# One more seven-product group in the first layer of the third half batch, with a newly written issue order

## The chip, the cores and the metric

One core of one Trainium2 chip. The metric is the time of one execution on the device in microseconds (us); lower is better. Work runs on TensorE (PE in the profile; PEld is its weight load), VectorE (DVE), ScalarE (ACT) and GpSimd (POOL); SyncE (SP) only issues transfers here.

## The reference

Attention over q, k, v of 4 x 8 x 768 x 64 (batch, heads, tokens, head size), in which a token sees the 8 first tokens (global) and itself with the 95 before it (local); then a feed-forward block with a squared ReLU on the 3072 tokens, with w_in 512 x 2048 and w_out 2048 x 512:

```python
scores = scale * np.matmul(q, k.transpose(0, 1, 3, 2))
bias = -slopes[:, None, None] * dist[None, :, :]
scores = np.where(keep, scores + bias[None], -1000000000.0)
a = softmax(scores)
x = np.matmul(a, v)          # then 3072 tokens x 512
h = np.maximum(x @ w_in, 0.0)
out = h * h @ w_out          # 3072 x 512, float32
```

## The kernel before

**Half batches.** The tokens are worked in eight half batches of 384 (H0 to H7). Each goes through the same stages: its q, k and v are loaded in tiles of 128 tokens; q and k are transposed so that the head size lies on the partitions; scores are made on TensorE (`score_unit`, L715, 64 rows of the array at a time), turned into exponentials on ScalarE (L728, ex) and masked on VectorE (phat); `attend` (L776) multiplies them with v and divides; the result tm is transposed by a transfer into xt (L801). Then the first layer (hps) and the second layer (yps, L1145 and L1059), whose sums y are stored. The stages of neighbouring half batches interleave: while H2 runs through its first layer, H3 makes scores and H4 is being loaded.

**First layer, two ways.** The 16 hidden blocks of 128 are made either plainly or in groups. A plain job (`layer1`, L822) makes one block: four matmuls over 384 columns (tokens), a relu out of the bank (L847 on ScalarE or L849 on VectorE), and a square for two blocks. A group (`layer1_group`, from L911) makes four blocks, two "near" and two "far", by seven block products in place of eight, after Strassen and Winograd: the columns are cut in halves of 192, the input channels in halves, and products p1 to p7 run on sums of weights (in_mix) and of tokens (x_mix) that are made ahead, once for all groups. A product is four matmuls over 192 columns (L925). Sums that several outputs share are held: `keep` copies a bank into a tile kept (L353 on ScalarE, L355 on VectorE). `give` makes hr from a bank: with a relu alone (L989 or L991), or adding a held sum first (add_relu, a custom instruction of VectorE, L983). In H2 groups are "seeded" (SEEDS): p1, p5, p6, p3, p7, p2, p4 in this order, with keep1 after p1, keep5 after p5, keep2 after p6, add_relu after p3 and p7, plain relus after p2 and p4, and a copy that writes keep1 back into p3's bank (seed) before p2 adds to it. So a seeded group has eight evacuations out of or into banks.

**Which jobs are in groups** is a string for each half batch, LAYER1 (L46). A letter of "abcdefg" is a product of group 3, of "ABCDEFG" of group 2, a digit of group 1; "s" is a plain job. Group 0's blocks are always plain.

**What sets the order.** One list of all engines' work, ORDER (L54 to L119), is read by `by_table` (L256): each word is an engine's letter and a number (p: the next TensorE job of that number, l: a load, others: any other operation), after a dot the banks, and after an @ the operation that a load must wait for. Every engine takes its work strictly in this order. So a wait holds up everything behind it on the same engine.

**Loads and transposes of q and k.** The transposes k<-sk and q<-sq are transfers that SyncE issues (`turn_by_dma`, L666 to L697, issue L670). Their sources sk and sq have one buffer each, so the loads of the next half batch (GpSimd's queue, `list_loads`, L491) wait for the transposes of the half batch before. The transpose that is issued first also waits for the last load of sq (x.last_load). The transpose of H4, for instance, must land before H4's first score. The values of a half batch also need a version vb in which the global tokens stand (`fix_v` L596, `fix_globals` L618); some of it is copied by transfers from SyncE, `vb<-v` (L625; L608 and L609 in `values_by_dma`).

```python
if not x.turns:
    behind(turn, x.last_load)            # turn_by_dma
for turn in halves[x.hb - 1].turns + (prev.xturns if AFTER[x.hb] else []):
    behind(dma, turn)                    # list_loads, tile 0 of sk
```

Of the kernel before, what the change touches and what calls it, by code (L numbers as in the profile page):

```python
# [45 lines left out]
LAYER1 = {2: "sasbcsdABCsesDEsFGfsgs", 3: "as123456b7cdsAeBCfgDsEFsG",  # L46
# [7 lines left out]
ORDER = """d1 s8 g2 a4 p0.0 a6 s10 d12 a0 d13 l1 d3 l4 l2 l3 d146 a26 d15 d20 a22 l0 a30 d9 d21 a18 d5 a17  # L54
a16 d14 a19 p1.12 a27 p5.34 a28 d11 l5 a29 p10.56 l9 d7 a23 l7 p3 l8 p4.7 l6 d32 a31 a24 d37 p6
d33 a34 p2.07 a39 d35 d36 p7 a40 p11 l10 a25 a41 p8.2 d43 p9.1 p13.34 a46 p12.20 d44 p17 l11 a42
d45 p14.1 d59 a47 l12 p15 d48 a52 p16.5 p24.7 p19.6 d51 p20.3 a49 l13 d55 a53 p18.1 p21.2 d64 l14
a50 p28.5 p23.64 d56 d38 a69 p27.7 d54 l16 p31.0 a57 p26.5 p34.32 a60 d72 l17 p29.6 d68 a61 p35.1
d70 p22.0 d58 l15 l18 a81 p25.4 p30.3 a85 p36.7 d65 a82 p39.16 a86 d71 a66 p32.02 a92 p33.47 d67
d63 p40.35 a77 d84 d91 p38.1 a78 d83 d62 d80 p37.4 l19 a73 d79 a74 p44.7 l22 p41.0 a93 d107 d87  # L60
d76 p47.2 a97 p52.6 p45.7 a89 l21 l23 d111 l20 l27 d96 a119 p48.3 a98 d75 l28 a101 p46.4 l29 p43.1
d110 p53.6 p42.2 d105 l30 d95 p50.5 p55.0 a103 l25 p49.4 d116 d94 a120 a112 p59.1 l24 a102 d88
d106 a90 p51.5 a108 d189 p60.2 a114 d100 a104 d99 p56.6 a113 d191 a122 p57.3 p65.7 d125 p54.4 d138
a117 p63.0 p62.5 a128 d121 a109 p58.1 d139 d129 d130 p61.3 a118 p67.7 d115 a132 d133 d272 a131
p70.4 a135 p71.2 a126 a142 p72.3 p69.0 d162 d127 p82.5 d190 a156 d192 a165 p66.1 a159 l31 a157
a160 p64.7 d205 d158 l26 d163 a123 d161 p84.0 d134 a140 d206 l36 d143 a166 p83.4 d207 a136 l35
d164 p81.6 a167 d187 a141 p85 l33 d124 a137 d186 p79.21 l34 l32 a184 d147 p88.37 p80.45 a178 p77.6
a195 p74.2 a181 d201 d202 a196 d204 p68.3 d203 a179 d151 a182 p73.4 d208 d180 a144 p90.7 l39 d183
a145 p86 a174 a168 d152 a169 p75.1 d154 p78.53 d153 p89.64 p87 a175 d148 a198 p100.2 a176 d155
a193 d150 p98.5 l38 p91.6 a185 d197 a199 d228 p76.3 a209 d177 a210 l37 p96.0 s229 a171 d200 p92  # L70
d172 d225 a173 s194 p93.5 s216 p94 d170 a188 d149 a211 p95.4 d236 s217 p105.1 d219 p97 d214 d237
d212 s220 p102.3 a240 p104 a245 p103.0 s226 d213 d238 a244 d227 d223 d221 p101 d218 p106 l45 a222
p99 l41@226 d246 a241 s215 d243 p109.54 p110.70 s224 l44 a234 p108.36 a251 d239 p111 d258 p118.5
a252 a248 a249 d250 p107 d273 p116.43 p113 a255 l42 p112 a268 l43@217 a256 d253 d230 d254 p119.6
l40 d257 d231 a269 p114.74 l47 p115.03 p124 a261 d274 l46 s235 p120 a283 d259 a264 d270 s275
p122.6 a262 p129.7 d280 p121.2 s242 s325 a265 d232 p127.0 d267 p126 d276 a287 p133.4 d285 d295
a286 d263 s324 p117.3 a290 d233 p130 p123.1 a278 p140 d266 a271 p132 d281 a307 p135 a291 p134.4
p128.2 d298 p136 d294 a279 p131.3 d300 s282 a299 s247 p137.6 a308 l48@324 a297 p138 a303 d323 d301
p139 p125.1 a302 p142 d288 d304 a292 p143.4 d305 a310 d311 p141.6 d326 l49 s296 a284 a312 p144.7
a309 d293 s289 l52 a306 p145.23 d313 p146.05 p147.14 l50 a327 d318 p148.6 a333 d433 d319 a322 l54  # L80
p149.2 a330 d336 a328 d314 l53 p151.16 d320 a331 p150.03 p152 a337 d329 l51 a338 d332 p157.5 a339
p153 d321 a341 d316 a344 a350 a334 p172.0 l65 d315 a342 d345 p159.3 d340 p158.1 p161 d335 a355
p164.2 a352 p155.4 d370 p154.6 p163 a347 d351 s371 p168.0 d395 p162 p169.1 d317 d358 a364 p156
a348 s398 p174.0 d356 a366 d343 a365 p171.4 d359 s399 l56 p177 p160.3 s277 d369 a378 p165 l55 a360
p167 d357 s346 d353 a363 p173.2 p166.4 a372 p178.5 a362 s260 d373 p175 d349 a361 p180 d375 p182.3
s374 p179 d382 a379 p176 p170 d380 p183 d385 p181.0 a381 s354 p184 a376 a383 s386 p185.5 d367 d400
a387 p186.23 d384 a389 p188.46 d388 l60@371 p187.01 a368 d377 a413 l59@354 p189.7 a406 d401 d405
l57 a414 d402 p190.4 a409 d404 l62 d403 a407 p191 a410 l63 p193.26 a417 d416 a418 p194.03 d415
p192.17 l61@386 p195 d476 d411 a419 s390 d391 a426 d408 l58 p196 p206.1 d393 a422 p198.0 d397 a420
p197.2 a434 d396 l74 a423 p219.7 d392 a432 d412 a427 d394 p210 d480 d429 p218.6 a445 d477 a462  # L90
d424 p208 a461 p204.4 d431 a448 p205.3 d421 p215.1 a444 p203.7 d443 p214 d442 a458 s491 l66 p199.6
p217.4 d457 p209 a451 p220 d435 a463 p202.7 d449 s492 d428 a441 p212.6 p224 a446 d454 p201 p207.3
a460 d481 d425 s436 a439 p200.7 d482 a471 p221 a447 p213 p216.6 d437 p222.5 d456 s438 d459 d478
# [1592 lines left out]
```

## Time and profile before

| | us |
|---|---|
| median of 3 runs | 201.74 (201.61 to 205.66) |
| the profiled execution | 201.98 |
| its span | 200.2 |
| PE / PEld busy | 191.8 / 160.8 |
| DVE / ACT / POOL busy | 177.7 / 146.3 / 66.6 |

The span is the time between the first and the last event in the profile; the execution has some microseconds around it. Busy time is summed per engine; PEld overlaps PE. The chain names the work that ended last, step by step back from the end. A window is a stretch of the span with the busy time of each engine in it. A row of a timeline gives start, duration, engine, line, operation, output<-input and, in brackets, the idle time of that engine before it and what ended it. SPq and POOLq are the queues in which SyncE and GpSimd issue transfers.

### The profile page before, as it was taken

Reading aid. Unit: us, or ns where it says so; the run is one execution under the profiler, and the core shown is the slowest. Engines: PE = TensorE matmul, PEld = TensorE weight load, DVE = VectorE, ACT = ScalarE, POOL = GpSimd, SP = SyncE. Lnnn points to the kernel's source line nnn. Section 1 sums busy time; section 2 is a strip of 40 time slices with the busy share of each in tenths; the row PEclk is TensorE's granted clock in tenths of the full one; section 3 lists DMA queues with packets and bytes.
Section 4 is the critical chain, followed back from the end, with each engine's and each line's share of the span. In section 5 each row is a group of like instructions: output and inputs, shape, how many; then the busy total and the mean of one; then the engine's idle time right before and its main releaser. Section 6 shows DMA issues by size and latency. Waiting matters only on the chain.

```text
span 200.2 us, 5881 instructions
## 1 busy us (share of the span) xinstructions
PE 191.8 (96%) x2349; PEld 160.8 (80%) x2349; DVE 177.7 (89%) x448; ACT 146.3 (73%) x310; POOL 66.6 (33%) x82
## 2 busy tenths in 40 slices
PE   7797999999999999999999998999999999999993
PEld 3575899856888687789877897889879899889992
DVE  6889778999995989999999997999999899899780
ACT  6899857998836679988888758987986866365311
POOL 5998537537102910970108700670000000000000
PEclk9999999999999999999999999999999999999999
DMA  5999999999998999999999995699734420020214
GB/s 161 177 149 181 198 181 171 207 194 155 149 224 89 143 123 243 134 149 105 272 119 93 152 140 114 146 150 155 199 75 142 105 75 2 0 108 0 108 52 157
DMA packets 106987, 27.52 MB, mean 137 GB/s; under 512 B 97104, under 2 KB 104016, under 8 KB 106960
## 3 DMA queue, kind: packets, MB, share of 16 engines
q0 software_dynamic: 74944, 13.11, 87.4%
q1 hardware_dynamic: 30816, 13.45, 32.1%
q10 hardware_dynamic: 1200, 0.59, 1.1%
q8 instruction: 18, 0.29, 0.7%
q14 instruction: 9, 0.07, 0.2%
HBM read 27.26 MB, written 6.29 MB: 168 GB/s over the span
## 4 chain that ended last, share of the span: by engine, by line
PE 76%; DMA 13%; POOL 6%; DVE 3%; issue 1%; SPq 0%; ACT 0%; POOLq 0%; DVEq 0%
PE yps L1145 29%; PE hps L822 17%; PE hps L925 17%; DMA w_in_sb<-in_moe_w_in_dram 5%; PE sp L715 4%; PE av L776 4%; PE yps L1059 4%; DMA q<-sq 3%; DMA xt<-tm 3%; DMA v<-in_v_dram 3%; POOL w_mix L491 2%; POOL v L491 2%; DVE hr L983 1%; PE trp L650 1%; POOL sk L491 1%
## 5 line engine op out<-in xcount | busy, mean ns | idle before, releaser
L822 PE MATMUL hps<-xt,w_in_sb 128*128 128x384 f16 (+2 forms) x336 | 45.3, 281 | 0.8 <-DMA w_in_sb<-in_moe_w_in_dram 0.8
L728 ACT ACTIVATE ex<-sp 128x512 f16<-128x512 f32 x66 | 35.3, 619 | 4.4 <-PE sp L715 3.6
L1145 PEld LDWEIGHTS <-h 128*128 128x128 f16 x376 | 34.1, 98 | 4.7
L822 PEld LDWEIGHTS <-w_in_sb 128*128 128x128 f16 x336 | 28.0, 98 | 8.7 <-DMA w_in_sb<-in_moe_w_in_dram 1.2
L1145 PEld LDWEIGHTS <-mixed 128*128 128x128 f16 x272 | 25.1, 98 | 3.1 <-DVE mixed L1110 0.2
L847 ACT ACTIVATE hr<-hps 128x384 f16<-128x384 f32 (+1 forms) x43 | 21.7, 548 | 7.6 <-PE hps L822 7.6
L983 DVE CUSTOM_DVE_ANT_0 hr<-hps,kept 128x384 f16<-128x384 f32 x49 | 25.8, 549 | 1.1 <-PE hps L925 0.7
L491 POOL DMA_DIRECT2D sq<-in_q_dram x19 | 17.0, 900 | 27.2 <-DMA xt<-tm 13.2
L353 ACT COPY kept<-hps 128x384 f32<-128x384 f32 x43 | 20.3, 491 | 7.9 <-PE hps L925 5.8
L353 ACT COPY y<-yps 128x256 f32<-128x256 f32 (+2 forms) x36 | 12.7, 381 | 18.0 <-PE yps L1145 16.5
L491 POOL DMA_DIRECT2D v<-in_v_dram x24 | 21.6, 918 | 12.1 <-DMA k<-sk 9.6
L491 POOL DMA_DIRECT2D sk<-in_k_dram x19 | 17.1, 902 | 25.2 <-DMA xt<-tm 9.4
L925 PEld LDWEIGHTS <-in_mix 128*128 128x128 f16 x272 | 23.0, 98 | 2.4 <-DVE x_mix L903 0.5
L925 PE MATMUL hps<-x_mix,in_mix 128*128 128x192 f16 x204 | 23.7, 247 | 0.2 <-DVE x_mix L903 0.2
L1145 PE MATMUL yps<-w_mix,h 128*128 128x256 f16 (+1 forms) x192 | 22.7, 264 | 0.0
L1145 PE MATMUL yps<-w_out_sb,h 128*128 128x256 f16 (+1 forms) x184 | 22.5, 268 | 0.0
L1145 PE MATMUL yps<-w_mix,mixed 128*128 128x256 f16 (+1 forms) x184 | 22.3, 268 | 0.0
L752 DVE TENSOR_TENSOR phat<-ex,mask 128x1024 f16<-128x1024 f16 (+1 forms) x36 | 21.0, 594 | 0.1
L1005 ACT ACTIVATE h<-hr 128x768 f16<-128x768 f16 x22 | 18.5, 848 | 1.2 <-DVE hr L983 0.7
L925 PEld LDWEIGHTS <-w_in_sb 128*128 128x128 f16 x204 | 17.4, 98 | 1.5
L861 ACT ACTIVATE h<-hr 128x768 f16<-128x768 f16 (+1 forms) x23 | 17.0, 768 | 1.7 <-DVE hr L849 0.9
L925 PE MATMUL hps<-xt,w_in_sb 128*128 128x192 f16 x136 | 15.8, 246 | 0.0
(110 smaller groups left out, 347.9 us busy)
## 6 DMA issues: line engine op xcount, KB each, us to landing
out_dram<-y SPq DMA_DIRECT2D x23, 256.0 KB, 2.6
v<-in_v_dram POOLq DMA_DIRECT2D x24, 128.0 KB, 6.4
sk<-in_k_dram POOLq DMA_DIRECT2D x19, 128.0 KB, 6.0
sq<-in_q_dram POOLq DMA_DIRECT2D x19, 128.0 KB, 5.0
w_in_sb<-in_moe_w_in_dram POOLq DMA_DIRECT2D x4, 512.0 KB, 10.2
w_out_sb<-in_moe_w_out_dram POOLq DMA_DIRECT2D x4, 512.0 KB, 10.5
y<-in_k_dram ACTq DMA_DIRECT2D x2, 256.0 KB, 4.8
y<-in_q_dram SPq DMA_DIRECT2D x2, 256.0 KB, 4.2
```

Source lines behind the costliest of these rows:

```text
L353: nc.scalar.copy(out=out, in_=in_)
L491: dma = nc.gpsimd.dma_start(out=dst, in_=src[x.b, :, r0 + t * P:r0 + (t + 1) * P, :] .rearrange("h p d -> p h d"))
L715: nc.tensor.matmul(sp[h][:, i, :], lhsT=lhsT, rhs=x.q[rows, r % HT, a, :], start=True, stop=True)
L728: nc.scalar.activation(out=st["ex"][:, h], in_=sp[h], func=AF.Exp, scale=scale)
L752: eng(e).tensor_tensor(out=x.phat[a][:, :, t0:t0 + n], op=ALU.mult, in0=st["ex"][:, :, i0:i0 + 2 * n].rearrange("p e (t b) c -> p e t (b c ...
L822: nc.tensor.matmul(st["ps"][:, i * n:(i + 1) * n], lhsT=w_in_sb[:, kk, m * P:(m + 1) * P], rhs=x.xt[:, kk, c0:c1], start=kk == 0, stop=kk ...
L847: nc.scalar.activation(out=o, in_=i, func=AF.Relu)
L861: nc.scalar.activation(out=h2, in_=hr, func=AF.Square)
L925: nc.tensor.matmul(st[name][:, i * HC:(i + 1) * HC], lhsT=left(i, kk), rhs=right(kk), start=fresh and i == kk == 0, stop=kk == KK - 1, ski ...
L983: nc.vector._custom_dve(TENSOR_ADD_SAT, out=hidden(which)[:, :, cols], in0=sums(name), in1=st[kept], s0=LARGEST, s1=0.0)
L1005: nc.scalar.activation(out=h2, in_=hr, func=AF.Square)
L1145: nc.tensor.matmul(st[bank_name][:, 0:n], lhsT=a(m), rhs=b(m)[:, cols], start=fresh and m == 0, stop=m == HK - 1, skip_group_check=not fresh)
```

## The change

H2 gets group 1 as well, in place of four plain jobs: 18 groups in all, for 17. The word for H2 now has three groups and four plain jobs. ORDER is written anew for all engines, one line longer, so all lines behind it have a number higher by one in the changed kernel (L822 is L823, and so on). 25 loads have an @ in it, where 8 had one. The core of the diff:

```diff
-LAYER1 = {2: "sasbcsdABCsesDEsFGfsgs", 3: "as123456b7cdsAeBCfgDsEFsG",
+LAYER1 = {2: "1a2b3csd4ABC5es6DEs7FGfsg", 3: "as123456b7cdsAeBCfgDsEFsG",
...
-ORDER = """d1 s8 g2 a4 p0.0 a6 s10 d12 a0 d13 l1 d3 l4 l2 l3 d146 a26 d15 d20 a22 l0 a30 d9 d21 a18 d5 a17
```

Counted over the kernel: matmuls of hps over 192 columns 476 to 504, over 384 columns 144 to 128; copies into kept 51 to 54, seed copies 2 to 3, add_relus 49 to 51, relus over 2 x 192 19 to 21, relus over 384 36 to 32. Several other copies move between ScalarE and VectorE.

**First place: GpSimd's loads of H4.** The rows are loads in order; the brackets name the semaphores that a load waits for. DMAHW0 to DMAHW7 are those of SyncE's transfers, taken in turn; DMASW0 to 7 are GpSimd's own. Before:

```order
L491 DMA sq<-in_q_dram 128x8x64 [waits DMASW3_49,DMAHW7_49,DMASW1_49,DMASW0_49]
L491 DMA sk<-in_k_dram 128x8x64 [waits DMAHW1_49,DMAHW6_49,DMASW4_49,DMASW2_49]
L491 DMA sq<-in_q_dram 128x8x64
L491 DMA sk<-in_k_dram 128x8x64
L491 DMA sq<-in_q_dram 128x8x64
L491 DMA sk<-in_k_dram 128x8x64 [waits DMASW5_49]
```

The changed kernel:

```order
L492 DMA sk<-in_k_dram 128x8x64 [waits DMAHW4_49,DMAHW6_49,DMASW4_49,DMAHW7_49,DMASW2_49,DMASW0_49]
L492 DMA sq<-in_q_dram 128x8x64 [waits DMAHW2_49,DMASW3_49,DMASW1_49]
L492 DMA sq<-in_q_dram 128x8x64
L492 DMA sk<-in_k_dram 128x8x64 [waits DMAHW0_49]
L492 DMA sk<-in_k_dram 128x8x64
L492 DMA sq<-in_q_dram 128x8x64 [waits DMASW5_49]
```

One load goes ahead of the gate in both. The gate of the second was an xt transpose of H2 (DMAHW1), and is now the copy vb<-v of H3 (DMAHW2), which SyncE issues behind it. The last load of sq, which the first transpose of H4 waits for, was the fourth of the loads behind the first, and is now the last.

**Second place: SyncE around the transposes of H7.** Before:

```order
L670 DMA_TRANSPOSE k<-sk 128x12x128 [waits DMASW7_49,DMASW5_49,DMAHW0_49,DMASW1_49,DMASW0_49]
L670 DMA_TRANSPOSE q<-sq 128x12x128 [waits DMASW6_49,DMAHW1_49,DMASW4_49,PE_49]
L1230 DMA out_dram<-y 128x512 [waits DMAHW2_49,DVE_49]
L1230 DMA out_dram<-y 128x512 [waits DMAHW3_49,Activation_49]
L801 DMA_TRANSPOSE xt<-tm 128x3x128 [waits DMAHW4_49,DVE_49,PE_49]
```

The changed kernel:

```order
L671 DMA_TRANSPOSE k<-sk 128x12x128 [waits DMASW6_49,DMASW5_49,DMAHW0_49,DMASW1_49,DMASW0_49]
L609 DMA vb<-v 96x520 [waits DMAHW1_49,DMASW2_49]
L610 DMA vb<-v 32x520 [waits DMAHW2_49]
L671 DMA_TRANSPOSE q<-sq 128x12x128 [waits DMASW7_49,DMAHW3_49,DMASW4_49,PE_49]
L1231 DMA out_dram<-y 128x512 [waits DMAHW4_49,DVE_49]
L1231 DMA out_dram<-y 128x512 [waits DMAHW5_49]
L802 DMA_TRANSPOSE xt<-tm 128x3x128 [waits DMAHW6_49,DVE_49,PE_49]
```

The two copies vb<-v stood behind the xt transposes that follow; now they stand between k and q, and the first of them waits for a v load (DMASW2).

**Third place: ScalarE in H2's first layer.** kept<-hps holds a sum, hps<-kept is the seed copy, hr<-hps a relu and h<-hr a square. Before:

```order
L353 COPY kept<-hps 128x384
L353 COPY hps<-kept 128x384
L353 COPY kept<-hps 128x384
L847 ACTIVATE hr<-hps 128x384 x2
L989 ACTIVATE hr<-hps 128x2x192
L353 COPY kept<-hps 128x384
L861 ACTIVATE h_1436<-hr 128x768
L353 COPY hps<-kept 128x384
L1005 ACTIVATE h_1436<-hr 128x768
```

The changed kernel:

```order
L354 COPY kept<-hps 128x384
L862 ACTIVATE h_1440<-hr 128x768
L990 ACTIVATE hr<-hps 128x2x192
L354 COPY hps<-kept 128x384
L1006 ACTIVATE h_1440<-hr 128x768
L354 COPY kept<-hps 128x384 x2
L990 ACTIVATE hr<-hps 128x2x192
L354 COPY kept<-hps 128x384
L848 ACTIVATE hr<-hps 128x384
L990 ACTIVATE hr<-hps 128x2x192
L354 COPY hps<-kept 128x384
```

Two of the three seed copies stay with ScalarE, the third goes to VectorE; between them stand more copies into kept and fewer plain relus.

More of the change, by code (lines that the diff above doesn't have):

```diff
@@ L59 @@
[L59 to L82, printed above, removed]
@@ L89 @@
[L89 to L93, printed above, removed]
-p211 a464 d489 l64 p223 d467 a469 p227.2 a484 a493 p229.7 d452 p225 d465 p230 s455 l70@455 d483
@@ L122 @@
+s729 d759 p369 a758 p363 p372 p373 p371.5 a757 d747 d742 s743 d751 d762 d761 d760 p376 p375 a768
+s763 d766 a769 s767 p366 a754 p374 s755 d764 s765"""
 class Op:
```

100 lines of the change are left out of this document (65 added, 35 removed).

## The prediction

> **What bounds the kernel now.** I read the page first: its span, the busy shares, then the chain that ended last by engine and by line.
>
> ```profile
> span 200.2 us, 5881 instructions
> PE 191.8 (96%) x2349; PEld 160.8 (80%) x2349; DVE 177.7 (89%) x448; ACT 146.3 (73%) x310; POOL 66.6 (33%) x82
> PE 76%; DMA 13%; POOL 6%; DVE 3%; issue 1%; SPq 0%; ACT 0%; POOLq 0%; DVEq 0%
> ```
>
> TensorE is busy for 191.8 of 200.2 us, and 76% of the chain is its work. A change can pay in two ways only: less matmul time, or less of the 8.4 us in which TensorE idles. The windows say where that idle time is. The columns are the stretch, its length, then PE, PEld, DVE, ACT and POOL busy, the granted clock, the DMA share and GB/s.
>
> ```profile
> 60.00:70.00 10.00, 10.00 (x121) 7.33 (x120) 7.60 (x19) 6.73 (x15) 6.35 (x8) 1.00 1.20 116
> 70.00:80.00 10.00, 10.00 (x116) 8.04 (x115) 9.00 (x24) 8.56 (x19) 0.65 (x1) 1.00 1.57 181
> 100.00:110.00 10.00, 9.84 (x120) 7.68 (x115) 9.83 (x25) 8.73 (x21) 4.29 (x5) 1.00 1.13 108
> 110.00:120.00 10.00, 9.85 (x139) 9.21 (x137) 9.79 (x26) 6.56 (x15) 3.63 (x5) 1.00 1.92 146
> 120.00:130.00 10.00, 9.43 (x117) 7.84 (x115) 8.62 (x22) 8.98 (x19) 3.21 (x4) 1.00 0.69 130
> ```
>
> Of the idle time most lies in the start, where the first weights land, and in the end, behind the last matmul; the change reaches neither, but for the last evacuation. In the middle three stretches miss 0.16, 0.15 and 0.57 us. The stretch in which the third half batch (H2; they are numbered from H0) has its first layer, 60 to 80, misses nothing: what is saved there is saved only if the evacuations and the transfers keep pace. The chain names what TensorE stood for in 110 to 130: a transposed q.
>
> ```profile
> 115.92 0.81 PE hps L925 x10
> 116.73 5.47 DMA q<-sq
> 122.20 0.14 issue
> 122.34 0.62 PE sp L715 x16
> ```
>
> The score runs of H6 start at 122.34, when a transpose that was issued at 116.73 has landed. So the transfers that bring q and k are the second limit: wherever TensorE comes to a score run early, or a transpose late, a stall appears.
>
> **The matmuls.** A plain job of the first layer is four matmuls over 384 columns, a block product four over 192. Two pieces of the chain inside the stage price them.
>
> ```profile
> 74.85 0.65 PE hps L822 x4
> 75.86 0.33 PE hps L925 x4
> ```
>
> Four plain jobs go, 4 x 0.65 = 2.60; seven products come, 7 x 0.33 = 2.31. The sums of weights and of tokens that they read are made already for every half batch that has groups, so nothing else is added. **-0.29.** Both kinds run here at the pace of their columns (0.163 and 0.082 per matmul), with their weight loads beside them. The Trainium skill ("TensorE: Matmul & The Clock Gate", section "Back-to-back issue gap") speaks against that: it puts streams of weight load and matmul at about 81 ns for 128 columns and about 131 ns for 512. An estimate by it, drawn straight between those two, is 89 ns for 192 columns and 114 for 384, so 28 x 89 - 16 x 114 would make the group dearer by 0.67 us; the rows above disagree with it.
>
> **The evacuations.** Four relus of 384 columns go. The new group, of the seeded kind that H2 uses, holds three sums (a copy each), adds two held sums with a relu, writes one held sum back and takes two plain relus: 8 for 4. The squares stay two.
>
> ```profile
> L353 ACT COPY kept<-hps 128x384 f32<-128x384 f32 x43 | 20.3, 491 | 7.9 <-PE hps L925 5.8 <-DVE hr L983 1.6
> L983 DVE CUSTOM_DVE_ANT_0 hr<-hps,kept 128x384 f16<-128x384 f32 x49 | 25.8, 549 | 1.1 <-PE hps L925 0.7 <-ACT h L1005 0.2
> L353 ACT COPY hps<-kept 128x384 f32<-128x384 f32 x2 | 1.0, 482 | 0.5 <-DVE hr L983 0.5
> L847 ACT ACTIVATE hr<-hps 128x384 f16<-128x384 f32 x29 | 13.4, 508 | 5.3 <-PE hps L822 5.3
> ```
>
> That is 3 x 0.491 + 2 x 0.549 + 0.482 + 2 x 0.508 less 4 x 0.508: +2.04 us on ScalarE and VectorE. In 60 to 80 ScalarE is idle for 3.27 + 1.44 and VectorE for 2.40 + 1.00 us, 8.11 together, which covers it; without that cover it would cost up to 2.04. What it cannot cover is order: with fewer plain jobs to put between, a product that goes into an occupied bank comes sooner after the copy that frees it. In the bank that is held, added to and written back, 0.491 + 0.549 + 0.482 = 1.52 us must pass between two products, and three or four other jobs of 0.33 to 0.65 stand there. Bounds 0 (each cover holds) and 0.3 (one of the six pieces of the chain misses by half of a 0.65 job); below nothing is out, since this stretch has no idle time to give. I take **+0.1**. The last evacuation of the kernel changes engine, from a ScalarE copy to a VectorE addition:
>
> ```profile
> 196.82 0.37 ACT y L353
> L1207 DVE TENSOR_TENSOR y<-yps,y 128x256 f32<-128x256 f32 x28 | 11.2, 417 | 2.5 <-ACT ex L728 1.4 <-PE yps L1145 1.0
> ```
>
> 0.417 for 0.37, **+0.05**, with the same store behind it.
>
> **The loads of H4.** These move most. GpSimd issues six loads of H4's q and k; the transposes into k and q follow on SyncE, and the first of the two waits for the last q load (line 666 on).
>
> ```profile
> 60.86 0.87 POOL L491 DMA_DIRECT2D sq<-in_q_dram  x1 [10.11 <-DMA q<-sq]
> 64.53 0.88 POOL L491 DMA_DIRECT2D sk<-in_k_dram  x1 [2.79 <-DMA xt<-tm]
> 67.12 0.90 POOL L491 DMA_DIRECT2D sq<-in_q_dram  x1
> 67.99 0.91 POOL L491 DMA_DIRECT2D sk<-in_k_dram  x1
> 61.10 1.64 SPq L625 DMA_DIRECT2D vb<-v  x1
> 72.02 2.06 SPq L670 DMA_TRANSPOSE q<-sq  x1
> 74.25 3.15 SPq L670 DMA_TRANSPOSE k<-sk  x1
> 81.31 0.78 PE sp L715 x24
> DMA to landing us min/median/max: 3.9/5.3/6.1
> DMA to landing us min/median/max: 1.8/2.7/4.1
> ```
>
> The last two rows are the landing times of the transposes (line 670) and of the copies vb<-v (line 625). Now: the second load is gated behind an xt transpose and starts at 64.53; the last q load starts at 67.12, and 4.90 later the q transpose goes; k follows at 74.25. Changed: the gate is the copy vb<-v, issued at 61.10, whose issue took 1.64 where a later copy of this kind, below, took 0.56; so I give it the longest landing, 4.1: 65.20. The last q load is now the fifth behind the gate; the fifth started 3.46 after it (67.99 - 64.53), so 68.66. The first transpose, now k, goes at 68.66 + 4.90 = 73.56 and q behind it, after 1.45 to 3.15 us of k (a row further down has the 1.45): 75.0 to 76.7. It lands 5.3 later, 80.3 to 82.0. TensorE wants it at 81.31 less what it has no longer to do before that: 0.29 saved, and work that the table moves behind the score run, by the count of its jobs 0.9: 80.1. The stall is 0.2 to 1.9, and 0 if the gate lands at the median of 2.7 (1.4 us sooner). Near the lower end, since k goes first here, as in the row with 1.45: **+0.8**, bounds 0 and 1.9.
>
> **H5 and H6.** SyncE now issues three xt transposes of H4 with one store between them, where three stores stood around them, and H6's loads sit behind an earlier gate. The wait at 122.34 is one row:
>
> ```profile
> 122.34 0.57 PE L715 MATMUL sp<-q,k 64*128 64x128 f16 x14 [0.57 <-DMA q<-sq]
> ```
>
> If the transpose comes 0.6 us sooner it is gone: **-0.57**, bounds -0.57 and 0. The 0.31 us missing in 100 to 120 (an x_mix and a v load) I halve, **-0.16**: the third v load of H5 becomes the last of its group, one issue of 0.9 us later, so a new wait can take their place.
>
> **H7.** Between its k and q transposes SyncE now has two copies vb<-v, which wait for H7's first v load; so the q transpose queues behind a v load, and behind it two stores and the xt transposes of H6.
>
> ```profile
> 131.11 0.92 POOL L491 DMA_DIRECT2D sq<-in_q_dram  x1
> 131.98 1.80 POOL L491 DMA_DIRECT2D v<-in_v_dram  x2
> v<-in_v_dram POOLq DMA_DIRECT2D x24, 128.0 KB, 6.4
> 136.02 1.45 SPq L670 DMA_TRANSPOSE k<-sk  x1
> 137.66 2.02 SPq L670 DMA_TRANSPOSE q<-sq  x1
> 147.35 0.56 SPq L608 DMA_DIRECT2D vb<-v  x1
> 147.96 0.58 SPq L609 DMA_DIRECT2D vb<-v  x1
> 142.89 0.78 PE sp L715 x24
> ```
>
> Before, q went at 137.66 and its score at 142.89. With loads as now, the v load lands at 131.98 + 6.4 = 138.38, two copies take 0.56 + 0.58 and a gap, and q goes at 139.6, 1.9 us later. It lands between 139.6 + 3.9 = 143.5 and 139.6 + 5.3 = 144.9, against 142.89: a stall of 0.6 to 2.0, less whatever earlier gates bring the loads forward (one issue each, 0.9). **+0.3**, bounds 0 and 1.8, nearer nothing because this estimate adds a median landing where TensorE has further jobs that the table can put ahead.
>
> **The sum** is made against the profiled execution, 201.98 us (span 200.2): -0.29 + 0.1 + 0.05 + 0.8 - 0.57 - 0.16 + 0.3 = +0.23, so 202.2 us there. That execution stands 0.24 above the median of the runs, 201.74; the forecast on the median's scale is **202.0 us**. All terms at their good ends make -0.29 + 0.05 - 0.57 - 0.31 = -1.12, 200.6; all at their bad ends -0.29 + 0.3 + 0.05 + 1.9 + 1.8 + 0.9 (the v load of H5) = +4.66, 206.4.
>
> **The rivals.**
> (a) The change pays in full: gates land early, the three old stalls go and none comes. 200.6 us. For it: both new waits are of a size with the landing spread (3.9 to 6.1). Against: TensorE never had more than about 2 us of reserve before a score run.
> (b) The input chain becomes the bound and the kernel gets slower. Place: the q transposes of H4 and H7. Price: 1.9 + 1.8, with the saving of 0.29 and the stall of H6 gone, 0.05 added: +2.9, 204.6 us; with H5's v load late too, 205.5. It decides from the point where the gate of H4 lands after about 65 and the v load of H7 after 138. For it: the issue rows of SyncE. Against: the two stalls are on one chain with the gates, and the first gives the transfers of the next half batches 1.9 us more.
> (c) ScalarE and VectorE become the bound in H2's stage: the 2.04 us of evacuations are not covered, because each waits in its engine's queue behind an exp or a square. +2.04 - 0.1 over the forecast: 203.9 us. Against: 8.11 us of idle time in that stretch.
> (d) Weight loads, not columns, pace the products: one takes 98 ns by the row below, so 28 x 0.098 - 16 x 0.163 = +0.14 in place of -0.29, and 202.4 us. The Trainium skill's rule above would be of this kind, at 202.9 by its figures. Against: the 0.33 for four products was measured with their loads.
>
> ```profile
> L925 PEld LDWEIGHTS <-in_mix 128*128 128x128 f16 x272 | 23.0, 98 | 2.4 <-DVE x_mix L903 0.5
> ```
>
> **How the numbers follow.** Forecast, that gains and new stalls nearly cancel (201.2 to 203.2): 0.49. (a) 0.27; (b) 0.13; (c) 0.07; (d) 0.04. The range 200.3 to 204.2 takes in (a), most of (c) and (d), and the lower part of (b). A measurement of this kernel can tell about 2% from no change, 4.0 us: below 197.7 or above 205.8. No case reaches 197.7, as only 0.29 of matmuls and 0.88 of stalls are to be had, so faster gets 0.02; slower needs (b) at its worst, 0.04.
>
> **What would show it.** In the changed profile: products at 0.33 per four and jobs at 0.65; 60 to 80 without idle PE; a wait of PE for q<-sq ahead of H4's first score run of about 0.8; none, or a shorter one, ahead of H6's; one of some tenths ahead of H7's, with the q transpose issued about two us after k's. I am wrong if PE is idle in the 60 to 80 stretch behind copies, if the first-layer stage of H2 lasts longer, or if the time is below 200.3, which would need a saving that I have not found.

## The result, and the profile after

The changed kernel is slower: median 208.41 us (207.19 to 209.29, 4 runs) against 201.81 (4 runs), a ratio of 1.031 [1.027, 1.036]. The forecast of 202.0 is missed by 6.4 us. Its profiled execution took 207.19 us with a span of 205.4, against 201.98 and 200.2: 5.2 us to find. That execution was the fastest of the four; what the median has above it, 1.2 us, no trace shows. Executions of some of the kernels below fall into two groups a few per cent apart; each ratio compares the lower group of both kernels, which holds at least half of the executions except in four runs: the new transfers under the old order of the engines (2 of 6), the first and the third run with the copy moved (5 of 13 and 2 of 12), and the changed kernel with only the group undone (1 of 4, so no ratio).

The page of the changed kernel, the rows that answer to those of before:

```profile
span 205.4 us, 5914 instructions
PE 194.9 (95%) x2362; PEld 163.8 (80%) x2362; DVE 177.3 (86%) x451; ACT 147.4 (72%) x311; POOL 66.8 (33%) x82
PE 43%; DMA 26%; DVE 14%; POOL 10%; issue 3%; SPq 1%; ACT 1%; POOLq 1%; DVEq 0%
```

PE's share of the chain fell from 76% to 43%, and DMA with POOL rose from 19% to 36%: what ended last now runs through loads and transposes. The windows say where (columns as in the prediction):

```profile
60.00:70.00 10.00, 9.84 (x124) 7.49 (x123) 7.82 (x22) 6.62 (x16) 5.84 (x7) 1.00 1.02 109
70.00:80.00 10.00, 10.00 (x124) 8.38 (x122) 9.40 (x25) 9.67 (x22) 2.81 (x4) 1.00 2.02 165
100.00:110.00 10.00, 7.08 (x83) 5.28 (x82) 6.43 (x15) 5.08 (x12) 3.77 (x5) 0.83 1.38 153
110.00:120.00 10.00, 9.78 (x111) 8.26 (x109) 9.45 (x24) 7.49 (x18) 5.05 (x6) 1.00 1.78 134
120.00:130.00 10.00, 10.00 (x133) 9.01 (x132) 9.42 (x25) 8.38 (x19) 0.00 (x0) 1.00 0.58 133
```

The stage of the new group, 60 to 80, is almost as full as before, and the 0.57 us that 120 to 130 missed is gone. The loss is in one stretch, 100 to 110: 2.92 us idle, and a granted clock of 0.83. TensorE's timeline there, and the first score runs of H4, H6 and H7 beside it:

```profile
80.51 0.34 PE L716 MATMUL sp<-q,k 64*128 64x128 f16 x6
...
103.46 0.23 PE L716 MATMUL sp<-q,k 64*128 64x128 f16 x2 [2.92 <-DMA q<-sq]
...
126.83 0.56 PE L716 MATMUL sp<-q,k 64*128 64x128 f16 x14
...
147.31 0.23 PE L716 MATMUL sp<-q,k 64*128 64x128 f16 x2
```

The first score run of H5 waits 2.92 us for a transposed q. Those of H4 (80.51), H6 (126.83) and H7 (147.31), which the prediction spoke of, have no bracket: they wait for nothing. Finer windows show what follows that stall:

```profile
104.00:105.00 1.00, 1.00 (x19) 0.83 (x13) 0.51 (x1) 0.90 (x2) 1.00 (x2) 0.95 0.91 260
105.00:106.00 1.00, 1.00 (x7) 0.69 (x6) 0.78 (x2) 1.00 (x3) 1.00 (x2) 0.50 2.36 47
106.00:107.00 1.00, 1.00 (x6) 0.72 (x5) 1.00 (x3) 1.00 (x3) 0.48 (x1) 0.50 0.39 9
107.00:108.00 1.00, 1.00 (x7) 0.72 (x5) 1.00 (x4) 0.52 (x2) 0.00 (x0) 0.50 2.05 170
108.00:109.00 1.00, 1.00 (x19) 0.67 (x19) 0.38 (x2) 0.00 (x0) 0.14 (x1) 0.84 2.22 158
```

About 1.4 us after work resumes, the clock is halved. PE is busy all the time and does half the work: the shortfalls add up to 0.05 + 0.50 + 0.50 + 0.50 + 0.16 = 1.71 us. With the stall that is 4.63 of the 5.2 us of this execution. It does not hold for the four alike: their mean granted clocks were 0.992 (207.19 us), 0.992 (207.73), 0.981 (209.09) and 1.000 (209.29), so the slowest of them lost nothing to the clock.

Why is q late? GpSimd's loads of H4 and H5 in the changed kernel (H5's from 86.37 on, its first v load):

```profile
65.04 1.75 POOL L492 DMA_DIRECT2D sq<-in_q_dram  x2 [1.58 <-DMA vb<-v]
...
68.50 0.91 POOL L492 DMA_DIRECT2D sq<-in_q_dram  x1
...
86.37 0.89 POOL L492 DMA_DIRECT2D v<-in_v_dram  x1 [5.04 <-DMA xt<-tm]
87.24 0.88 POOL L492 DMA_DIRECT2D sk<-in_k_dram  x1
...
89.84 0.91 POOL L492 DMA_DIRECT2D sq<-in_q_dram  x1
```

SyncE's transfers beside them:

```profile
74.15 1.43 SPq L671 DMA_TRANSPOSE k<-sk  x1
75.68 2.71 SPq L671 DMA_TRANSPOSE q<-sq  x1
...
80.37 1.24 SPq L802 DMA_TRANSPOSE xt<-tm  x1
...
89.95 0.54 SPq L1231 DMA_DIRECT2D out_dram<-y  x1
90.59 0.45 SPq L1076 DMA_DIRECT2D out_dram<-y  x1
97.75 1.41 SPq L671 DMA_TRANSPOSE k<-sk  x1
99.27 1.78 SPq L671 DMA_TRANSPOSE q<-sq  x1
```

And the same places before, GpSimd first, then SyncE:

```profile
80.29 0.88 POOL L491 DMA_DIRECT2D v<-in_v_dram  x1 [9.65 <-DMA k<-sk]
...
83.76 1.80 POOL L491 DMA_DIRECT2D sq<-in_q_dram  x2
```

```profile
79.37 11.35 SPq L801 DMA_TRANSPOSE xt<-tm  x3
91.72 1.43 SPq L670 DMA_TRANSPOSE k<-sk  x1
```

The chain of waits ties them together:

```profile
62.26 2.23 DMA vb<-v
...
80.37 5.71 DMA xt<-tm
...
89.84 7.76 DMA sq<-in_q_dram
```

The changed list makes the first v load of H5 wait for an xt transpose of H3 (an @ that before had not). Issued at 80.37, behind H4's transposes and a store in SyncE's queue, that transpose lands 5.71 later, and GpSimd stands 5.04 us. Four loads of q and k stand behind it. The last q load goes at 89.84, where its like went at about 84.6, and takes 7.76 to land; the k transpose goes at 97.75 for 91.72 and q behind it.

### The profile page after: what moved, and what is told of

Same layout as the page of the kernel before. It is cut to its first block, busy times and chain, and to the rows that moved or that the text cites. A ratio compares the mean times of both kernels' runs of the same rounds, so it can differ in the third digit from the quotient of the medians.

```text
span 205.4 us, 5914 instructions
## 1 busy us (share of the span) xinstructions
PE 194.9 (95%) x2362; PEld 163.8 (80%) x2362; DVE 177.3 (86%) x451; ACT 147.4 (72%) x311; POOL 66.8 (33%) x82
## 4 chain that ended last, share of the span: by engine, by line
PE 43%; DMA 26%; DVE 14%; POOL 10%; issue 3%; SPq 1%; ACT 1%; POOLq 1%; DVEq 0%
PE yps L1146 16%; PE hps L823 12%; PE hps L926 10%; DMA v<-in_v_dram 9%; DMA xt<-tm 9%; DMA sq<-in_q_dram 4%; POOL sk L492 3%; POOL sq L492 3%; DMA vb<-v 3%; POOL v L492 2%; DVE mixed L1111 2%; DMA q<-sq 2%; POOL w_mix L492 2%; PE av L777 1%; DVE w_mix L590 1%
## 5 line engine op out<-in xcount | busy, mean ns | idle before, releaser
L823 PE MATMUL hps<-xt,w_in_sb 128*128 128x384 f16 (+2 forms) x320 | 43.1, 278 | 0.2 <-DMA xt<-tm 0.2
L823 PEld LDWEIGHTS <-w_in_sb 128*128 128x128 f16 x320 | 26.7, 98 | 6.6
L1146 PEld LDWEIGHTS <-mixed 128*128 128x128 f16 x272 | 25.9, 101 | 4.6 <-issue 0.8
L354 ACT COPY kept<-hps 128x384 f32<-128x384 f32 x48 | 22.2, 485 | 10.1 <-PE hps L926 7.4
L984 DVE CUSTOM_DVE_ANT_0 hr<-hps,kept 128x384 f16<-128x384 f32 x51 | 27.1, 552 | 2.7 <-PE hps L926 2.4
L354 ACT COPY y<-yps 128x256 f32<-128x256 f32 (+2 forms) x41 | 15.0, 382 | 17.5 <-PE yps L1146 16.2
L926 PEld LDWEIGHTS <-in_mix 128*128 128x128 f16 x288 | 24.4, 98 | 2.2 <-issue 0.4
L1146 PE MATMUL yps<-w_mix,mixed 128*128 128x256 f16 (+1 forms) x184 | 23.8, 279 | 0.2 <-DVE y L356 0.2
L926 PE MATMUL hps<-xt,w_in_sb 128*128 128x192 f16 x144 | 17.0, 246 | 0.0
L862 ACT ACTIVATE h<-hr 128x768 f16<-128x768 f16 (+1 forms) x21 | 15.6, 761 | 0.9 <-DVE hr L850 0.7
```

Of the source, the lines that this page charges most:

```text
L354: nc.scalar.copy(out=out, in_=in_)
L823: nc.tensor.matmul(st["ps"][:, i * n:(i + 1) * n], lhsT=w_in_sb[:, kk, m * P:(m + 1) * P], rhs=x.xt[:, kk, c0:c1], start=kk == 0, stop=kk ...
L862: nc.scalar.activation(out=h2, in_=hr, func=AF.Square)
L926: nc.tensor.matmul(st[name][:, i * HC:(i + 1) * HC], lhsT=left(i, kk), rhs=right(kk), start=fresh and i == kk == 0, stop=kk == KK - 1, ski ...
L984: nc.vector._custom_dve(TENSOR_ADD_SAT, out=hidden(which)[:, :, cols], in0=sums(name), in1=st[kept], s0=LARGEST, s1=0.0)
L1146: nc.tensor.matmul(st[bank_name][:, 0:n], lhsT=a(m), rhs=b(m)[:, cols], start=fresh and m == 0, stop=m == HK - 1, skip_group_check=not fresh)
```

## The experiments

In the words of ORDER below, s is a SyncE transfer, a the work of ScalarE and d that of VectorE. The wait of a load is called its gate. Line numbers differ by a few between these kernels. The first question was whether the two @ of H5's loads are the cause by themselves.

**The gate of the v load off.**

```diff
- l56@299
+ l56
```

> The changed kernel, without the wait of H5's first v load for an xt transpose of H3 (the word l56@299 becomes l56). The last q load of H5 keeps its own wait for the same transpose. Theory: that one wait holds the five q and k loads queued behind it on GpSimd until 86.37 us, so the last q load goes at 89.84, the q transpose at 99.27, and TensorE stands for 2.92 us before H5's first score and then runs 3.4 us at half clock. Without it the last q load goes about 3.5 us sooner, at 86.4, the q transpose lands at about 99.8, TensorE wants it at 100.5: no stall, no drop of the clock, and the time falls by 2.9 to 3.2 and 1.7 us from 208.4 to about 203.5. Rival (the new group's evacuations and the rest of the order are what costs): the time stays within 1 us of 208.4.

Median 206.26 us, ratio 1.023 [1.016, 1.029]. The wait of H5's score is gone, and another came 14 us earlier:

```profile
89.69 0.81 PE L926 MATMUL hps<-xt,w_in_sb 128*128 128x192 f16 x4 [1.65 <-DMA xt<-tm]
```

```profile
89.00:90.00 1.00, 0.30 (x3) 0.29 (x4) 0.26 (x1) 0.10 (x1) 0.00 (x0) 0.87 2.43 155
90.00:91.00 1.00, 1.00 (x9) 0.94 (x7) 0.96 (x4) 0.00 (x0) 0.00 (x0) 0.50 2.65 154
```

The first layer now waits for xt, again with half a clock behind it: without the gate the loads go out while xt transposes are in flight, which would explain it but was not tried apart. So the gate decides where the lateness falls, and is not all of it.

**Both gates of H5 off.** The last q load had one too.

```diff
- l56@299  l52@299
+ l56      l52
```

> As the run before, and the wait of H5's last q load for the same xt transpose is taken away too (l52@299 becomes l52). Theory: all loads of H5 go in a row from 79.2 on, the last q load at about 84.8 as in the kernel before (84.6), the q transpose lands at about 98.9; with 1.5 us of reserve nothing more is gained than by the first wait alone: 202.5 to 203.5 us. Rival (loads and transposes get in each other's way, which is what the waits were to prevent): the transposes of H3 and H5 land later than in the run before and the time is 1 us or more above it.

206.05 us, 1.020 [1.011, 1.029]: no different from one gate off. A wait of 1.37 us for xt stands in the place of the 1.65, this time with the clock at 1.00 throughout.

**The gate alone, in the kernel before.**

```diff
- l52
+ l52@296
```

> The kernel before, with only this added: H5's first q load waits for an xt transpose of H3 (l52 becomes l52@296), so that five q and k loads stand behind that wait, as in the changed kernel. Theory: the wait alone makes most of the loss: the loads of H5 start again at 84 to 86 us rather than at 82, the last q load goes 3 to 4 us later than 84.6, the q transpose lands at about 102 where TensorE wants it at 99.6: a stall of 2 to 3 us and, if it is long enough, a drop of the clock of 1.7 us more: 204 to 206.5 us. Rival (the loss belongs to the group and the rest of the new order): 202 us, as before.

0.999 [0.994, 1.005]: no change. The gate held for 0.55 us only, since in the order of before that xt transpose goes out ahead of the loads and lands soon:

```profile
82.82 0.88 POOL L491 DMA_DIRECT2D sq<-in_q_dram  x1 [0.55 <-DMA xt<-tm]
```

A wait in the list costs what its releaser is late, and nothing as such. The theory that the gates of H5 are the cause falls; the question became what makes their releaser late.

**The stall kept, but TensorE busy in it.** Thirteen matmuls of 512 columns ahead of H5's first score, into a bank that the score then overwrites.

```diff
+if x.hb == 5 and not getattr(x, "busy_wait", False):
+    x.busy_wait = True
+    for _ in range(13):
+        nc.tensor.matmul(sp[0].rearrange("p i c -> p (i c)"), lhsT=w_in_sb[:, 0, 0:P],
+                         rhs=w_in_sb[:, 0, 0:512], start=True, stop=True)
```

> The changed kernel with 13 matmuls of 128x512 on w_in_sb ahead of H5's first score run, into the bank that this run then overwrites (2.8 us of extra work that the result does not use). They fill the time in which TensorE otherwise stands. Theory: the late q transpose and then the drop of the clock are two separate costs; with TensorE busy in the wait the stall stays as long (now as filler) but the clock stays at 1.00 between 104 and 109 us, and the time is about 1.7 us below the changed kernel's, 206.7 us. Rival (the clock costs nothing of its own, the loss is the stall and the work behind it): 208.4 us, no change.

```profile
102.52 2.97 PE L714 MATMUL sp<-w_in_sb 128*128 128x512 f16 x13
```

```profile
104.00:106.00 2.00, 2.00 (x29) 1.07 (x29) 1.93 (x4) 0.00 (x0) 0.39 (x1) 1.00 0.74 183
```

The clock stays at 1.00. That fits idle time as what halves it, but does not show it: in a run further down TensorE idles for 2.61 us at the same place and the clock stays at 1.00 too. The time did not follow: 208.46 us, 1.034 [1.027, 1.041], as slow as the changed kernel. This execution's TensorE has waits of 1.2 and 0.9 us for ex and 1.0 for xt that the changed kernel's has not. Whether these took all of the 1.71 was not settled.

**Stores behind the transposes.** If the releaser is late because SyncE issues it behind stores, two xt transposes of H3 ahead of two stores should bring it forward; first with the gates of H5, then without.

```diff
- d294 s242 ... a288 p140.1 s299 ... p155 d321 s291
+ d294 s299 s291 s242 ... a288 p140.1 ... p155 d321
```

> The changed kernel with its waits as they are, and only the xt transposes a3 and a2 of H3 moved ahead of the two stores. Theory: a3, which the loads wait for, is issued 0.7 us earlier and still lands behind two loads that are in flight, at about 85.4 rather than 86.1; the q transpose of H5 comes 0.7 us sooner, the stall ahead of H5's first score shrinks from 2.9 to about 2.2 us: 206.5 to 207.7 us, less if the clock no longer drops (205). Rival (the place of the stores decides alone): 203 us.

205.50 us, 1.017 [1.010, 1.025]. The stall of H5's score went, and a new one of 2.65 us stands at H4's second run. The rows of ScalarE and TensorE:

```profile
86.77 0.37 ACT L352 COPY y<-yps 128x256 f32<-128x256 f32 x1 [3.04 <-DMA out_dram<-y]
```

```profile
87.70 0.50 PE L714 MATMUL sp<-q,k 64*128 64x128 f16 x6 [2.65 <-ACT ex L727]
```

The stores that were put back free y buffers later; a copy into y waits 3.04 us on ScalarE, the exponentials stand behind it, and the scores wait for their banks. Here too the clock is 0.50 after it (88 to 90).

> The changed kernel with both waits of H5's loads taken away, as in the second run, and two words of the order moved: SyncE issues the xt transposes a3 and a2 of H3 right behind a1, ahead of the two stores that stood between them. Theory, as the first two runs left it: the late transfer is a choice of two. With the waits H5's q transpose is late, without them xt a2 of H3, which then stands behind the loads (issued at 83.58, landed at 90.97, where the kernel before has 80.68 and 86.52). With a2 at about 81 it lands at about 87, TensorE wants it at 88, and H5's loads are early: neither stall, 202.5 to 203.5 us. Rival (evacuations of the new group, or another part of the order, are what makes it slow): 205 us or more, with stalls of TensorE that name ScalarE or VectorE.

208.60 us, 1.033 [1.024, 1.042], with 3.9 us of the same wait for ex. The edit trades one stall for another; a failed repair.

**The group undone.** LAYER1 for H2 as before, its four plain jobs, relus and squares put in the places of the group's work; all else as in the changed kernel, and once more with the transposes moved as above.

```diff
-LAYER1 = {2: "1a2b3csd4ABC5es6DEs7FGfsg",
+LAYER1 = {2: "sasbcsdABCsesDEsFGfsgs",
```

> The changed kernel with only the group undone, as in the run before, and the waits and xt transposes as in the changed kernel. Theory: the group has no part in the loss; the wait for H5's q transpose stays, since it is set by transfers, and takes up the 0.3 us: 208 to 208.7 us. Rival (the group delays what the transposes wait for): 204 us or less, with no stall ahead of H5's first score.

209.72 us (205.98 to 210.18), no ratio. In the traced execution, of 210.18 us, the wait for q<-sq at H5's score is there, 2.8 us. So the order that came with the group makes that stall without the group too.

> The kernel of the first run in this set (waits off, xt first), with the group undone: in the places of group 1's seven products four plain jobs of H2, with four relus and two squares in the places of its evacuations; all else in the same order. Theory: with the transfers in time the group is worth its 0.29 us of matmuls: this run comes out 0.3 us above the run with the group, 202.8 to 203.8. Rival (the group's chains of evacuations cost more than it saves): 0.5 us or more below the run with the group.

207.90 us, 1.028 [1.023, 1.033], with the gates of H5 off, as in the run of 208.60 us; 4.9 us of waiting for ex, the failed repair again.

**Whose order?** The next kernels keep the changed order of TensorE, VectorE and ScalarE, and give GpSimd and SyncE from H4's loads on the order and waits of before (l and s words moved); then the converse, the kernel before with the new transfers; then the first with the group undone.

```diff
- ... l40@229 s215 a252 l43@215 l45 l42@226 p114.21 d230 a261 s224
+ ... l45 l41@226 s224 l44 l42 l43@217 l40 l47 l46 s235
```

> The changed kernel with the order of the transfers undone: TensorE, VectorE and ScalarE have every instruction and its order from the changed kernel, group 1 of H2 included; GpSimd's loads and SyncE's transposes, copies and stores stand, from H4's first load on, in the order of the kernel before, with its waits. Theory: the order of the transfers makes the loss; the q transpose of H5 is in at about 99 us, xt a2 of H3 at about 87, and the time is that of the kernel before within 1.5 us: 200.5 to 203 us. Rival (the engines' new order, or the group in it, makes the loss): 205 us or more.

204.79 us, 1.012 [1.005, 1.018]. That lies between the two forecasts: the transfers' order carries some 60% of the loss (3.1% to 1.2%), and 1.2% stays with the engines' own new order.

> The converse: TensorE, VectorE and ScalarE as in the kernel before, without the group; GpSimd's loads and SyncE's transfers, from H4's first load on, in the order of the changed kernel, with its waits. Theory: the loads of H5 wait again for xt a3 of H3 (landing at about 85 to 86), their last q load goes at about 89, the q transpose lands at 101 to 103 us where TensorE wants it at 99.7: a stall of 2 to 3 us and a drop of the clock, 205 to 208 us. Rival (the engines' order makes the loss): 201.5 to 203 us.

211.70 us, 1.032 [1.024, 1.042]: the new transfers alone, under the old order of the engines, cost the kernel before all that the whole change cost.

> The first run of this set with the group undone as well: four plain jobs, four relus and two squares in the places of group 1's products and evacuations in H2, the transfers those of the kernel before. Theory: with no late transfer near it the group is worth its 0.29 us of matmuls: 0.2 to 0.5 us above the run with the group. Rival (the seeded chains of copies cost more than 0.29): this run is below the run with the group.

205.82 us, 1.016 [1.009, 1.022] with the group undone, 1.012 with it: the intervals overlap, so the 0.29 us of the group is not resolved.

**Which part of it?** Cut at H5's q transpose: old transfers up to it and new ones behind, then new up to it and old behind.

> The changed kernel, with the transfers in the order of the kernel before (waits too) from H4's first load up to H5's q transpose, and in its own order behind that. Theory A (what is wrong lies ahead of H5's score: H4's and H5's loads, their waits, the stores between the xt transposes): as with all transfers undone, 203 to 205 us. Theory B (the order behind H5 loses as much): 206 us or more.

204.66 us, 1.015 [1.011, 1.019]. TensorE's longest waits behind the start are 1.5 us at 70.4, for a copy into kept that comes up again below, and 1.2 at 108.5, for an xt transpose.

> The converse: the changed kernel, its own transfers up to H5's q transpose, those of the kernel before behind it. Theory A: the stall ahead of H5's first score and the drop of the clock stay, 206.5 to 208.5 us. Theory B: 204 to 206 us.

208.80 us, 1.033 [1.028, 1.039], with the stall of the changed kernel:

```profile
103.74 0.23 PE L714 MATMUL sp<-q,k 64*128 64x128 f16 x2 [2.61 <-DMA q<-sq]
```

Here the granted clock is 1.00 through the stall and behind it, and the time is no better for it.

So with TensorE's new order the four mixtures read 1.012 (old, old), 1.015 (old, new), 1.033 (new, old) and 1.031 (new, new): what lies ahead of H5's q transpose makes the difference, and what lies behind it makes none that can be told.

> The kernel before with the changed kernel's order of transfers from H4's first load on, as in the run that lost the whole 3.2%, but without the two waits of H5's loads for xt a3 of H3. Theory A (these two waits make the loss): 202 to 203.5 us. Theory B (the loss is spread over the new order of the transfers, the waits only choose who is late): 205 us or more, with a wait of TensorE for an xt transpose or for a later q or v in the place of the one for H5's q.

```diff
- l56@299  l52@299
+ l56      l52
```

Made on the converse kernel: 210.39 us, 1.042 [1.038, 1.046], slower still. A second time the gates of H5 are not the cause. The trace bears out Theory B: H5's score waits for nothing, but H4's first score waits 0.32 us for q (81.97) and H7's 1.03 (149.27), and the other long waits are 1.10 for a v load (117.62) and 0.82 for a sum of tokens (113.26). So under the old order of the engines the same transfers are late in other places.

**One word.** The earliest new wait ahead of that point that holds a load up is the one on the second load of H4, for the copy vb<-v of H3.

```diff
- l43@215
+ l43
```

> The changed kernel without the wait of H4's first q load for the copy vb<-v (l43@215 becomes l43), the term of the forecast that was largest. By the forecast: H4's loads go 1.5 us sooner and a stall ahead of H4's score of 0.8 us goes with them: 207.6 us. By the trace, which shows no such stall: no gain there, but H4's v and transposes and with them xt a3 of H3 and H5's loads come up to 1.5 us sooner, the stall ahead of H5's score shrinks to 1.5 us and the clock holds: 205 us. If neither: 208.4 us.

203.95 us, 1.008 [1.005, 1.012]: one word is worth 2.3% of the 3.1%, that is 0.023 x 201.8 = 4.6 us by the ratios, and 4.1 by the two traced spans (205.4 and 201.3). The expectation was a shorter stall; in this trace H5's score waits for nothing and the clock is 1.00 throughout. GpSimd and SyncE in that kernel:

```profile
63.63 1.80 POOL L490 DMA_DIRECT2D sq<-in_q_dram  x2
...
84.31 0.88 POOL L490 DMA_DIRECT2D v<-in_v_dram  x1 [2.96 <-DMA xt<-tm]
...
87.78 0.91 POOL L490 DMA_DIRECT2D sq<-in_q_dram  x1
```

```profile
73.47 2.23 SPq L669 DMA_TRANSPOSE k<-sk  x1
...
79.93 1.24 SPq L800 DMA_TRANSPOSE xt<-tm  x1
...
92.52 2.23 SPq L669 DMA_TRANSPOSE k<-sk  x1
```

Step by step, the changed kernel against this one:

| | this | changed | later by |
|---|---|---|---|
| second load of H4 | 63.63 | 65.04 | 1.41 |
| k transpose of H4 | 73.47 | 74.15 | 0.68 |
| xt transpose of H3, issued | 79.93 | 80.37 | 0.44 |
| first v load of H5, released by it | 84.31 | 86.37 | 2.06 |
| last q load of H5 | 87.78 | 89.84 | 2.06 |
| k transpose of H5, released by it | 92.52 | 97.75 | 5.23 |

The lateness shrinks on its way to the xt transpose, and grows twice, each time between an issue and its landing: 0.44 to 2.06, and 2.06 to 5.23. By which way it reaches that transpose is not decided: SyncE issues almost without a gap from H4's k transpose on, but the chain of the changed kernel goes through H4's last v load (issued at 71.11, landed 6.43 later) and the work of VectorE behind it, and the two ways end within 0.2 us of each other. Nor is the 1.41 us a measure against the kernel before, whose second load of H4, held by an xt transpose, went at 64.53, 0.51 us ahead of the changed kernel's: there no load of H5 waits for an xt transpose. It takes the late loads of H4 and the wait at H5 together.

In the changed kernel two stores of 256 KB go out at 89.95 and 90.59, on the heels of the last q load of 89.84; in this one at 90.67 and 91.33, some 3 us behind it. That fits the Trainium skill ("DMA: Bandwidth & Descriptors", section "Queues, rings and completion order"), which says that each DMA engine goes round the queues that have work for it, a packet from each. From that one would expect a load to have less of the engines while another queue is full. Four more traces go the same way. With the first store within 0.7 us of H5's last q load, the k transpose goes 8.3 us behind that load (TensorE busy in the stall: 91.18 and 99.51) and 7.6 (new transfers up to H5: 90.47 and 98.08). With the store some 4 us behind the load, it goes after 5.2 (xt first, gates on: 89.10 and 94.33) and 4.8 (the last run with the group undone, below: 87.02 and 91.77). That these stores are what stretches the load is still argued from rows, since no run moved the stores alone.

The longest wait of TensorE that is left in this kernel behind the start is in H2's stage; the others are 0.3 us or so each. TensorE, and VectorE ahead of it:

```profile
69.64 0.82 PE L924 MATMUL hps<-x_mix,in_mix 128*128 128x192 f16 x8 [1.04 <-DVE kept L354]
```

```profile
68.37 0.75 DVE L902 TENSOR_TENSOR x_mix<-xt,x_mix 128x384 f16<-128x384 f16 x2 [1.50 <-DMA xt<-tm]
69.04 0.55 DVE L354 COPY kept<-hps 128x384 f32<-128x384 f32 x1
```

The copy that empties a bank stands behind two sums of tokens, and these wait for an xt transpose until 68.37. The same place in the changed kernel:

```profile
67.39 0.75 DVE L904 TENSOR_TENSOR x_mix<-xt,x_mix 128x384 f16<-128x384 f16 x2 [0.62 <-DMA xt<-tm]
```

There xt is 0.98 us sooner, with the loads of H4 going 1.41 later. So the removed wait had a use: early loads cost some 1 us here.

**That copy first, too.**

```diff
- l43@215 ... d258 p116.74 d231 a268 d233 d273 d253 d232 d254
+ l43 ... d258 p116.74 d273 d231 a268 d253 d232 d254 d233
```

The copy (d273) goes ahead of the two sums of tokens, and the second of these (d233) three places later.

> As the run without the wait of H4's first q load (ratio 1.008), and on VectorE the copy keep1 of group 3 in H2 is moved ahead of the two x_mix sums in front of it, which wait there for xt a3 of H2 (VectorE idle for 1.50 us, TensorE then for 1.04). Theory: what was left of the loss, 1 to 1.7 us, is this stall; TensorE now waits only for the x_mix sum that the next product reads: about 0.7 us less, 203.2 us, ratio 1.004. Rival (the rest of the loss is spread over small waits at the end): no change, 203.9 us.

1.001 [0.998, 1.005], but the median of all executions is 206.70 us. The traced execution took 208.74 us, so what the copy's move does is read from the next run, which has it too.

> The first run of this set with the group undone: four plain jobs, four relus and two squares of H2 in the places of group 1's products and evacuations. Theory: where no transfer is late, the group saves its 0.29 us of matmuls: 0.2 to 0.5 us above the run with the group. Rival (its evacuations cost more): below it.

The same with the group undone: 202.62 us, 1.002 [1.000, 1.005]. The ratios differ by 0.1%, so by them the group is worth nothing that can be told. The medians of all executions do differ, 206.70 with the group and 202.62 without; why was not tried. In this trace the wait of 1.04 us has become one of 0.32 for the sum of tokens, TensorE has no wait for a transfer behind the start, and k of H5 goes at 91.77, as in the kernel before.

> The first run of this set, with H7's q transpose ahead of the two copies vb<-v on SyncE. By the forecast's term for H7 (0.3 us, at most 1.8): 0.3 us less, 202.9 us. By the changed kernel's trace, in which no wait for H7's q shows: no change, 203.2 us, or more if the copies come late now.

```diff
- p243.2 l73 s574 ... a539 p258.5 s578 s525
+ p243.2 l73 s578 s574 ... a539 p258.5 s525
```

H7's q transpose ahead of the two copies vb<-v: 1.002 [0.995, 1.008], with a median of all executions of 206.38 us. The H7 term is not resolved. Since none of these versions beats the kernel before, none is offered in its place.

## Why the prediction was wrong, and where it was right

**The matmuls: the price was right, its worth is not resolved.** Products and plain jobs in the chain of the changed kernel still cost 0.33 and 0.65 per four:

```profile
111.79 0.65 PE hps L823 x4
113.31 1.32 PE hps L926 x16
```

The three pairs with the group made and undone (1.012 and 1.016, 1.001 and 1.002, and 1.033 and 1.028 where both wait for ex) differ by less than their intervals.

**The evacuations: covered, and the order priced about right.** The 60 to 80 stretch lost 0.16 us, all of it behind one copy into kept, against +0.1. Its upper bound of 0.3 would not hold with earlier loads: in the run with the gate of H4 off the same copy cost 1.04. The term looked at the chain of copies in a bank, and not at what else stands ahead of a copy in VectorE's queue.

**The loads of H4: right delay, in part by luck, and wrong place of payment.** The gate opened at 65.04 for 65.20, and the k and q transposes went at 74.15 and 75.68, near the forecast. That the gate came out was luck: the copy vb<-v went at 62.26, 1.16 us later than the 61.10 that was taken over from before, and landed in 2.23 us for the 4.1 assumed. The +0.8 was wrong: TensorE came to H4's score at 80.51 for the 80.1 assumed, and nothing waited, so q had landed within 4.83 us of its issue, for the 5.3 assumed. What failed is that the term ended there. The delay went on, past H4's scores, to the xt transpose that releases H5's loads.

**H5 and H6: the step that failed.** It said "the third v load of H5 becomes the last of its group, one issue of 0.9 us later". That load never mattered. The step overlooked the first v load of H5, which got a wait on an xt transpose, with four loads of q and k behind it; so it could not see that 1.41 us at the second load of H4, against the kernel without that wait, would be 5.23 us at the k transpose of H5. It gave -0.16 where the trace has +2.92. The run with the one word at H4 taken out shows that this lateness is most of the loss (1.031 to 1.008). The other half was right: the 0.57 us ahead of H6's score went.

**The clock: not in the sum at all.** Each stall was priced at its length. In the traced execution this one was followed by 1.71 us more at a halved clock; other executions were as slow with the full clock, so that this is a cost of its own is not shown.

**H7 and the end.** The q transpose went 3.3 us behind k (142.81 against 139.50), more than the 1.9 forecast, and H7's score still did not wait, because TensorE came some 4.4 us later than before; with H5 repaired the term could not be resolved. The wait can come, though: with the new transfers under the old order of the engines H7's q held TensorE for 1.03 us. The last addition took 0.42, the +0.05 as forecast.

**The rivals.** Rival (b), the input chain as the bound, is what happened, with the right gate (it decides, it says, where "the gate of H4 lands after about 65") and the wrong places, H4 and H7 for H5, and 204.6 us for 208.41. Its chance of 0.13 came from weighing H4's reserve of about 2 us, and from leaving its own last sentence, that the first stall "gives the transfers of the next half batches 1.9 us more", as an argument against. That holds if the wait is on TensorE; here TensorE ran on and only the transfers were late.

**What stays open.** Which transfers stretch the two landings; when a stall is followed by the halved clock, and what that costs in the end; why taking the wait away at H5 brings a wait for xt (the loads beside xt in flight, argued); and what the busy wait's 1.71 us went into.

## What to carry to other kernels

Follow a late transfer past its first reader: a queue that runs in order hands its lateness to the next gate, and a gate in front of five loads is paid by the last of them. When a list gains waits, read for each what releases it and when, then what stands behind it; a wait costs its releaser's lateness, as one word at H4 (4.6 us) and one at H5 (nothing, in the kernel before) show. A stall of TensorE can be followed by a halved clock: name that as a term with a range, here 0 to 1.71 us for a stall of 2.6 to 2.9, and do not count on it.

## What the runs showed of the hardware that was not expected

**A short stall can halve the clock.** After stalls of 2.92 us (changed kernel), 2.65 (transposes first) and 1.65 (v load's gate off) the granted clock was 0.50; after 1.37 (both gates off) it stayed at 1.00, and so it did after 2.61 (new transfers up to H5's q). So the length of the stall alone does not decide it. In the changed kernel the shortfall of 1.71 us is 3.4 us at half clock. The Trainium skill ("TensorE: Matmul & The Clock Gate", section "Part 1: The HAM clock gate") gives windows of about 3.4 us that run freely, and the half clock after at least one idle window. The length of the slow spell agrees with that window; the idle time needed does not, since 1.65 us was enough here. With the stall filled with matmuls the clock was 1.00 as well, in one trace.

**Landing times spread widely.** The xt transpose that released H5's loads took 5.71 us in the changed kernel, where the median of its kind is 3.4 (2.3 to 6.8, in the kernel before as well). A q load took 7.76 for a median of 5.5:

```profile
sq<-in_q_dram POOLq DMA_DIRECT2D x19, 128.0 KB, 5.5
xt<-tm SPq DMA_TRANSPOSE x24, 3.4
```
